# Attention and two gated MLPs on one core: odd query tiles transposed from key 0, groups of seven, and a planner given new priorities and buffer counts

## The chip, the cores and the metric

The kernel runs on one core of a Trainium2 chip. The metric is the device time of one execution in microseconds; the median of several executions is compared. All inputs and outputs are float32.

## What is computed

The first part is attention with a top-32 mask: 4 batches, 8 heads, 576 positions, head size 64. The result, 2304 tokens of 512 features, goes through two gated MLPs (512 to 1536 and back), one after the other.

```python
scores = scale * np.matmul(q, k.transpose(0, 1, 3, 2))
kth = np.partition(scores, -top_k, axis=-1)[..., -top_k:-top_k + 1]
attn = exp(where(scores >= kth, scores, -1e9) - max); attn /= sum + 1e-9
x = matmul(attn, v)                       # (B, H, S, D) -> (B*S, H*D)
x = (silu(x @ w_gate) * (x @ w_val)) @ w_out          # MLP 1
x = (sigmoid(x @ w_gate2) * (x @ w_val2)) @ w_out2    # MLP 2
```

## The kernel before

The 36 tiles of 64 queries (nine for each batch) are dealt to six chunks of 4, 5, 6, 7, 7 and 7 tiles. For each chunk comes `attention(c)` and then `moe(c)`, which runs both MLPs on the chunk's tokens, transposed (features on partitions, 256 to 448 tokens as columns). A chunk that crosses a batch boundary has two segments: chunk 3 has 3 + 4 tiles, chunk 4 has 5 + 2, chunk 5 has 7 of one batch.

**Attention.** Heads are taken in pairs. A unit of work is one pair of query tiles (m = 2, 128 queries, head 0 and head 1 beside each other in the row of `p`) or, where a group has an odd number, one single tile (m = 1), whose 128 partitions are 64 queries of head 0 and below them 64 queries of head 1. For each unit TensorE makes scores (`ps_s`), ScalarE copies them to `s`, VectorE finds the 32nd largest value of each row by four `max` and three `match_replace` steps (`top_full`), exponentials and mask follow (`row_tile`), and the rows are divided by their sum (`norm`, ScalarE or GpSimd). Then `turned` transposes the probabilities `p` in blocks of 128 keys on TensorE into `ps_t` (two buffers), and ScalarE copies them into `pt`, of which there is one buffer, nine blocks of 128 keys by up to 64 x `GMAX` queries. `pv` then multiplies `pt` with the values, ten matmuls for one group of up to `GMAX` tiles, and ScalarE copies the result to `x32`.

For a single tile, `turned` is called three times. The first two calls transpose four blocks each, head 0's from key 0 and head 1's from key 64, and each is copied out by one instruction that takes only that head's 64 columns of the block. The third call turns the last 64 keys of head 0 and the first 64 of head 1, 64 columns wide, with two small copies; one of these already reads partitions 0 to 63 and writes 64 to 127. There are 16 single tiles (chunks 1, 3, 4 and 5, four head pairs each) and 64 double ones. `groups` cuts a segment of seven tiles into 2 + 5, since `GMAX` is 6.

**MLPs.** Chunk 0 uses float32 weights (mode N), which `decode` rebuilds from packed 64-bit input (`wr` buffers, result `wf`, also stored to DRAM as `sw`). The other chunks (mode P) load `sw` into `raw` and split it into a high and a low part, `w` (ScalarE or GpSimd for the high one, GpSimd or VectorE for the low one); each product is then three matmuls (both parts of `w` with `xh`, and the high part of `w` with `xl`).

**Order of the work.** Nothing is scheduled by hand. Each operation is handed to `Plan` with its engine (or a choice of engines), an estimated duration, its inputs, the buffers that it needs, and a priority (smaller goes first, then program order). `Plan.run` simulates the engines with these numbers, and the order in which it starts the operations is the order in which they are issued, on every engine and on SP's DMA queue. Buffers of a ring are handed out in program order. The scores of chunk 5 are made early, in the time of chunks 0 and 1 (`early`, `E_IN`), stored to DRAM and loaded later. The constants ahead of the program are priorities (`P_...`, `NA`, `NP`, `HP`, `E_DMA`) and buffer counts (`WR`, `RAW`, `SIL`, `H32`, `WK`, `KR_RING`).

Of the kernel before, what the change touches and what calls it, by code (L numbers as in the profile page):

```python
# [18 lines left out]
P = 128  # L19
B, H, S, D = 4, 8, 576, 64  # L20
# [19 lines left out]
E_STEP = 0  # L40
E_SKIP = 2
E_LAST = 1
E_IN = [2, 1, 0, 0, 0, 0]
BEFORE = [1, 0, 0, 0, 0, 0]
WR = 4
P_CUT = 0
E_PRIO = 2
E_DMA = 5
SP = 4
WU = 3  # L50
KE = 2
HP = 2
DL = 6
NA = 0
NP = 1
P_ROUND = 5
P_MASK = 1
P_DEC = 2
P_MM = 3
P_QK = 2  # L60
P_K = 1
P_PT = 2
P_PV = 1
P_EX = 2
P_S = 1
P_X = 1
P_HH = 2
P_HL = 0
PT = 1
RAW = 3  # L70
WF = 16
W = 4
SIL = 3
H32 = 2
WK = 2
E_RING = 2
P_RING = 2
Q_RING = 2
K_RING = 2
KS_RING = 1  # L80
QS_RING = 1
KR_RING = 2
V_RING = 2
GMAX = 6
S_RING = 4
DMA_LAT = 2010.0
DEBUG = False
# [199 lines left out]
def act(n):  # L287
    return 5 + 1.18 * n
# [27 lines left out]
def attn_moe_kernel(ctx: ExitStack, tc, qT, kT, qD, kD, vL, wall, outT):  # L316
# [25 lines left out]
    def phase_pool(n, name, bufs):  # L342
# [16 lines left out]
        "x32": ring("x32", [P, NPAIR, S], F32, 1),  # L359
        "sil": ring("sil", [P, HW], F32, SIL),  # L360
        "h32": ring("h32", [P, HW], F32, H32),
        "s": ring("s", [P, 2, 2, 288], F32, S_RING),
        "st": ring("st", [P, 36], F32, 2 * S_RING + 2),
        "wk": ring("wk", [P, 2, 288], F32, WK),
        "e": ring("e", [P, S], F32, E_RING),
        "p": ring("p", [P, 2 * S], F32, P_RING),
        "pt": ring("pt", [P, 9, 64 * GMAX], F32, PT),
        "v": ring("v", [P, 10, D], F32, V_RING),
# [6 lines left out]
    for n in SIZES:  # L375
        g = sum(SIZES[:len(chunks)])
        segs = []
        for b in range(g // QT, (g + n - 1) // QT + 1):
            lo, hi = max(g, b * QT), min(g + n, (b + 1) * QT)
# [5 lines left out]
    for n in sorted(set(PHASE)):  # L385
# [3 lines left out]
        if "N" in kinds:  # L389
            T = max(SIZES[c] for c in mine if MODES[c] == "N") * 64  # L390
            specs.update(xn=([P, ND, T], F32, 2), hn=([P, NF, T], F32, 1), wr=([P, 512, 2], I32, WR),
                         wf=([P, 512], F32, WF), wu=([P, 512], I32, WU), wg=([P, 128], I32, 2))
# [5 lines left out]
        if kinds - {"N"}:  # L398
            specs["raw"] = ([P, 512], F32, RAW)
            specs["w"] = ([P, 2, 8, P], F32R, W)  # L400
        if n == 0:
            specs.update(q=([P, S], F32, Q_RING), k=([P, S], F32, K_RING))
        if n == PHASE[-1]:
            Q = 128 * max(x for y in chunks[NAT:] for _, _, x in y[2])
            specs.update(qr=([P, Q], F32, 1), qs=([P, Q], F32R, QS_RING), kr=([P, S], F32, KR_RING),
                         kh=([P, S], F32R, 2 * KS_RING), kl=([P, S], F32R, 2 * KS_RING))
# [21 lines left out]
    def f32(ap):  # L428
        return ap.bitcast(F32)

    def new(name, label=""):
        r = R[name]
        return Gen(r, f"{name if isinstance(name, str) else name[0]}_{len(r.gens)}{label}")
# [12 lines left out]
    def split_ops(hi, lo, raw, n, uses, deps, pa, pp, allocs=(), lo_raw=None, lo_hi=None):  # L446
# [7 lines left out]
        def f_lo(eng):  # L454
            (nc.gpsimd if eng == "pool" else nc.vector).tensor_sub(lo(), (lo_raw or raw)(), lo_hi() if lo_hi else f32(hi()))  # L455
        a = op({"act": (act(n), pa), "pool": (76 + n, pa + HP)}, 0, f_hi, deps=deps, uses=uses, allocs=allocs)
        b = op({"pool": (pool_tt(n), pp), "dve": (dve(n), DL)}, 0, f_lo, deps=[a], uses=list(uses) + list(allocs),
# [102 lines left out]
    def early():  # L560
        for c, on in enumerate(EARLY):
            for p in range(int(on)):
                for b, q0, n_s in chunks[c][2]:
                    kg, qg = new(("ke", 0)), new(("qe", 0))
                    lds = [load(kg, kT[b * NPAIR + p], n_bytes=P * S * 4, prio=E_DMA),
                           load(qg, qT[b * NPAIR + p, :, q0 * 64:(q0 + n_s) * 64], dst=lambda g, n=n_s: g[:, :n * 64],
                                n_bytes=P * n_s * 256, prio=E_DMA)]
                    for _, jp, m in pairs(q0, n_s):
# [3 lines left out]
    def early_pair(c, p, b, j, kg, qg, lds, o, m):  # L572
# [4 lines left out]
        def st():  # L577
            nc.sync.dma_start(scr, sg[:, :m])
        scr_s[p, b, j] = scr, op("dma", dma(P * S * 4 * m), st, deps=done, uses=[sg], prio=E_DMA, lat=DMA_LAT)

# [30 lines left out]
    def stacked_scores(sg, kq, o, m):  # L611
        keys, qs, deps, n = kq
        done = []
        for x in range(2):
            psg = new("ps_s")

            def qk(x=x, psg=psg):
                take(psg)
                for h in range(2):
                    at = o * 64 + (h * n * 64 + h * 64 * (n % 2) if m == 2 else 0)  # L620
                    for i in range(2):
                        nc.tensor.matmul(psg[:, h, :288], qs[:, at:at + P], keys[h][i][:, x * 288:x * 288 + 288],  # L622
                                         start=(i == 0), stop=(i == 1))
            a = op("pe", pe(4, 288), qk, deps=deps, uses=[qs] + [g for y in keys for g in y], allocs=[psg], prio=P_QK)
            done += to_sbuf(sg, [sg], psg, a, x, m, P_S)
        return done
# [78 lines left out]
    def segment(c, p, b, q0, n_s, x32g, col):  # L705
        bp = b * NPAIR + p
        kg = kq = None
        if p >= int(EARLY[c]) and (c > NAT or c == NAT and p >= NATP):
            kq = stacked(bp, q0, n_s)
        elif p >= int(EARLY[c]):  # L710
            kg, qg = new(("k", 0)), new(("q", 0))
            lds = [load(kg, kT[bp], n_bytes=P * S * 4, prio=1),
                   load(qg, qT[bp, :, q0 * 64:(q0 + n_s) * 64], dst=lambda g: g[:, :n_s * 64],
                        n_bytes=P * n_s * 256, prio=1)]
        vg = new("v")
        v_ld = load(vg, vL[bp], n_bytes=P * 2560, prio=3)
        adds = []
        off = 0
        for n in groups(n_s):
            ptg = new("pt")  # L720
            pt_ops = []
            for jp in range((n + 1) // 2):
                m = min(2, n - 2 * jp)
                pg, sg = new("p"), new("s")
                o = off + 2 * jp
                if kq is not None:
                    done = stacked_scores(sg, kq, o, m)
                elif kg is None:
                    done = [score_load(sg, m, *scr_s[p, b, q0 + o])]
                else:  # L730
                    done = score_ops(sg, [sg], kg, qg, lds, o, m, P_QK, P_S)
                norms = [row_tile(sg, new("st"), done, e, pg, BEFORE[c]) for e in range(m)]
                tiles[0] += 1
                if tiles[0] > E_SKIP:
                    step(E_IN[c])
                for k3 in range(3):
                    pt_ops += turned(pg, norms, ptg, 2 * jp * 64, k3, m)
            adds.append(pv(ptg, pt_ops, vg, v_ld, n, p, x32g, col))
            off += n
            col += n * 64  # L740
        return adds
# [7 lines left out]
    def row_tile(sg, stg, a, e, pg, before):  # L749
# [58 lines left out]
        y = op("dve", 75, inv, deps=[y], uses=[stg], prio=P_MASK)  # L808
        return op({"act": (act(S), NA), "pool": (700, NP)}, 0, norm, deps=[y], uses=[pg, stg])

# [24 lines left out]
    def turned(pg, norms, ptg, c0, k3, m):  # L835


        tg = new("ps_t")
        h = 64 * (m - 1) + 64
        if k3 < 2:  # L840
            o = [64 * k3 + (S * k3 if m == 2 else 0) + i * P for i in range(4)]
            deps = [norms[k3 if m == 2 else 0]]
            parts = [(lambda: ptg[:, 4 * k3:4 * k3 + 4, c0:c0 + h],
                      lambda: tg[:, :, 64 * k3:64 * k3 + 64] if m == 1 else tg[:], 4 * h)]
            width = P
        elif m == 2:
            o, deps, width = [512], norms, P
            parts = [(lambda: ptg[:, 8, c0:c0 + h], lambda: tg[:, 0], h)]
        else:
            o, deps, width = [512, 0], norms, 64  # L850
            parts = [(lambda e=e: ptg[64 * e:64 * e + 64, 8, c0:c0 + h],
                      lambda e=e: tg[:64, e, 64 * e:64 * e + 64], h) for e in range(2)]

        def tr():
            take(tg)
            for i, a in enumerate(o):
                nc.tensor.transpose(tg[:width, i], pg[:, a:a + width], ident)  # L857
        t = op("pe", 5 + pe(len(o), 128), tr, deps=deps, uses=[pg], allocs=[tg], prio=P_PT)
        out = []
        for dst, src, n in parts:  # L860
            def cp(dst=dst, src=src):
                take(ptg)
                nc.scalar.activation(out=dst(), in_=src(), func=AF.Copy)  # L863
            out.append(op("act", act_ps(n), cp, deps=[t], uses=[tg], allocs=[ptg], prio=P_PT))
        return out

    def pv(ptg, pt_ops, vg, v_ld, n, p, x32g, col):
# [4 lines left out]
        def go():  # L872
            take(og)
            for i in range(5):
                for h in range(2):
                    nc.tensor.matmul(og[64 * h:64 * h + 64, :W], vg[:, 8 + h if i == 4 else 4 * h + i],  # L876
                                     ptg[:, 8 if i == 4 else 4 * h + i, :W], start=(i == 0), stop=(i == 4))
        a = op("pe", 200 + 10 * max(W / 1.2 + 3, 110), go, deps=pt_ops + [v_ld], uses=[ptg, vg], allocs=[og], prio=P_PV)

# [16 lines left out]
    def moe(c):  # L896
# [20 lines left out]
        for moe_i in range(2):  # L917
            hs_g = [new(("hn", ph))] if nat else [new(("hh", ph)), new(("hl", ph))]
            h_ops = {}
            for f in range(NF):  # L920
# [4 lines left out]
                for gv in range(2):  # L925
                    blk, wg, w_ready = w[gv]
                    for o, n in halves:
# [5 lines left out]
                        deps = w_ready + ([y for x in x_ready for y in x] if f == 0 else [])  # L933
                        m = op("pe", pe_t(n), mm, deps=deps, uses=[wg] + xs, allocs=[pg], prio=P_MM)
                        if gv == 0:
# [22 lines left out]
                        def mul(pg=pg, sg=sg, h32=h32, n=n, moe_i=moe_i):  # L958
# [6 lines left out]
                                                lambda h32=h32, n=n: h32[:, :n], n,  # L965
                                                [h32], [v], P_HH, P_HL, allocs=[hh, hl])
            if moe_i == 0:
# [3 lines left out]
            for hs in range(12):  # L971
# [4 lines left out]
                for o, n in halves:  # L976
# [7 lines left out]
                    deps = w_ready + [prev] + [y for d in range(4) for y in h_ops[4 * s3 + d, o]]  # L984
                    m = op("pe", pe_t(n), mm, deps=deps, uses=[wg] + hs_g, allocs=[pg], prio=P_MM)
                    accs[o] = pg, m
# [96 lines left out]
```

## Time and profile before

| | |
|---|---|
| median of 3 executions | 1300.52 us (1300.29 to 1302.53) |
| the profiled execution | 1302.69 us |
| its span, first to last instruction | 1300.9 us |
| mean granted TensorE clock | 0.978 |
| busy: TensorE (PE) / its weight loads (PEld) | 1241.8 us / 1062.6 us |
| busy: VectorE (DVE) / GpSimd (POOL) / ScalarE (ACT) | 1110.6 us / 862.7 us / 837.5 us |

PE, PEld, DVE, ACT and POOL are the names in the profile; SP is the engine that issues all DMAs. L857 is line 857 of the kernel. TensorE's busy time is modelled, since matmuls overlap; its weight loads run beside them.

### The profile page before, as it was taken

What the parts mean: (1) busy time and instruction counts of PE and PEld (TensorE: products, weight loads), DVE (VectorE), ACT (ScalarE), POOL (GpSimd) and SP (SyncE); (2) the same over time, 40 slices, a digit from 0 to 9 for tenths busy, and PEclk for the clock granted to TensorE, in tenths of its full rate; (3) what the DMA queues carried; (4) which work ended last, traced back from release to release, by engine and by line L of the source; (5) the groups of instructions that cost most, each with busy time, mean ns of one, the idle gap of its engine ahead of it and who ended that gap; (6) DMA issues with size and microseconds to landing.
All of it is one profiled execution on the core that took longest, in us unless ns stands there. A gap on an engine that the chain in (4) does not pass through costs nothing.

```text
span 1300.9 us, 21941 instructions
## 1 busy us (share of the span) xinstructions
PE 1241.8 (95%) x7240; PEld 1062.6 (82%) x7240; DVE 1110.6 (85%) x2345; ACT 837.5 (64%) x1662; POOL 862.7 (66%) x853
## 2 busy tenths in 40 slices
PE   4677999998999999999999999999999999999998
PEld 1233677877899999999998988989889889999998
DVE  7899999899999989999999999999999965364441
ACT  6876889777877878767778676656555543332331
POOL 5633465646999999978898886777677654333341
PEclk9867999999999999999999999999999999999999
DMA  8772788885444454453444343445444223333332
GB/s 283 264 263 97 227 277 284 268 297 191 160 133 152 147 162 142 142 165 122 133 136 158 123 150 101 132 144 163 136 145 139 86 90 120 119 106 105 113 98 69
DMA packets 101202, 206.34 MB, mean 159 GB/s; under 512 B 12256, under 2 KB 21856, under 8 KB 101088
## 3 DMA queue, kind: packets, MB, share of 16 engines
q1 hardware_dynamic: 101088, 204.94, 48.7%
q8 instruction: 57, 0.93, 0.3%
q14 instruction: 57, 0.47, 0.1%
HBM read 173.05 MB, written 31.85 MB: 158 GB/s over the span
## 4 chain that ended last, share of the span: by engine, by line
PE 73%; DVE 9%; ACT 7%; DMA 4%; POOL 4%; issue 2%; SPq 0%; ACTq 0%; POOLq 0%; DVEq 0%
PE ps_m L911 58%; PE ps_t L857 5%; PE ps_v L876 5%; DVE st L824 3%; DMA wr<-in_wall_dram 3%; DVE wk L826 3%; PE ps_s L639 3%; PE ps_s L622 2%; DVE p L789 2%; DMA raw<-sw 1%; ACT wf L469 1%; ACT wg L484 1%; ACT s L649 1%; POOL w L455 1%; POOL wu L488 1%
## 5 line engine op out<-in xcount | busy, mean ns | idle before, releaser
L455 POOL TENSOR_TENSOR w<-raw,w 128x512 fp32r<-128x512 f32 x309 | 419.5, 1368 | 41.2 <-ACT w L450 31.9
L911 PE MATMUL ps_m<-xh,w 128*128 128x448 f32 (+2 forms) x1920 | 405.2, 353 | 0.4 <-POOL w L455 0.4
L911 PEld LDWEIGHTS ps_m<-xh,w 128*128 128x128 f32 x1920 | 337.5, 189 | 20.5 <-issue 1.5
L824 DVE MAX8 st<-wk 128x8 f32<-128x576 f32 x432 | 313.3, 745 | 0.0
L450 ACT ACTIVATE w<-raw 128x512 fp32r<-128x512 f32 x263 | 163.6, 628 | 172.4 <-PE ps_m L911 122.1
L911 PE MATMUL ps_m<-xl,w 128*128 128x448 f32 (+2 forms) x960 | 218.5, 349 | 0.0
L826 DVE MATCH_REPLACE8 wk<-st,wk 128x576 f32<-128x576 f32 x288 | 212.8, 739 | 0.0
L911 PE MATMUL ps_m<-hh,w 128*128 128x448 f32 (+2 forms) x960 | 201.7, 352 | 0.0
L452 POOL TENSOR_SCALAR w<-raw 128x512 fp32r<-128x512 f32 x97 | 64.1, 661 | 176.4 <-DMA raw<-sw 87.2
L911 PEld LDWEIGHTS ps_m<-xl,w 128*128 128x128 f32 x960 | 172.6, 188 | 9.7
L911 PEld LDWEIGHTS ps_m<-hh,w 128*128 128x128 f32 x960 | 168.6, 188 | 10.1 <-issue 0.9
L789 DVE SCALAR_TENSOR_TENSOR p<-s,st,e 128x576 f32<-128x576 f32 x128 | 145.3, 1135 | 0.0
L857 PE MATMUL ps_t<-ident,p 128*128 128x128 f32 (+1 forms) x736 | 116.2, 288 | 12.0 <-ACT p L802 9.0
L857 PEld LDWEIGHTS ps_t<-ident,p 128*128 128x128 f32 (+1 forms) x736 | 89.7, 145 | 42.5 <-ACT p L802 19.1
L863 ACT ACTIVATE pt<-ps_t 128x512 f32<-128x512 f32 (+3 forms) x256 | 106.6, 438 | 21.6 <-PE ps_t L857 20.0
L940 ACT ACTIVATE sil<-ps_m 128x448 f32<-128x448 f32 (+3 forms) x144 | 70.1, 487 | 70.5 <-PE ps_m L911 69.5
L824 DVE MAX8 st<-s 128x8 f32<-128x576 f32 x144 | 106.8, 743 | 8.0 <-ACT s L649 8.0
L455 DVE TENSOR_TENSOR w<-raw,w 128x512 fp32r<-128x512 f32 x51 | 53.9, 1058 | 65.5 <-POOL w L452 45.6
L911 PE MATMUL ps_m<-hl,w 128*128 128x448 f32 (+2 forms) x480 | 109.3, 349 | 0.0
L826 DVE MATCH_REPLACE8 wk<-st,s 128x576 f32<-128x576 f32 x144 | 106.5, 739 | 0.0
L802 ACT ACTIVATE p<-p,st 128x576 f32<-128x576 f32 x116 | 89.4, 771 | 22.2 <-DVE st L797 21.5
L777 ACT ACTIVATE e<-s,st 128x576 f32<-128x576 f32 x128 | 99.1, 774 | 3.1 <-POOL st L760 1.3
(70 smaller groups left out, 1804.5 us busy)
## 6 DMA issues: line engine op xcount, KB each, us to landing
raw<-sw SPq DMA_DIRECT2D x360, 256.0 KB, 2.8
wr<-in_wall_dram SPq DMA_DIRECT2D x72, 512.0 KB, 4.8
sw<-wf SPq DMA_DIRECT2D x72, 256.0 KB, 4.6
kr<-in_kD_dram SPq DMA_DIRECT2D x38, 288.0 KB, 2.9
v<-in_vL_dram SPq DMA_DIRECT2D x32, 320.0 KB, 3.3
ss<-se SPq DMA_DIRECT2D x12, 576.0 KB, 3.8
s<-ss SPq DMA_DIRECT2D x12, 576.0 KB, 4.2
out_dram<-h SPq DMA_DIRECT2D x12, 224.0 KB, 2.5
```

The source lines that it names most:

```text
L450: nc.scalar.activation(out=hi(), in_=raw(), func=AF.Copy)
L455: (nc.gpsimd if eng == "pool" else nc.vector).tensor_sub(lo(), (lo_raw or raw)(), lo_hi() if lo_hi else f32(hi()))
L777: nc.scalar.activation(out=eg[:], in_=src(), func=AF.Exp, bias=stg[:, 32:33], scale=SCALE)
L789: nc.vector.scalar_tensor_tensor(out=o, in0=src(), scalar=stg[:, 31:32], in1=eg[:], op0=ALU.is_ge, op1=ALU.mult, accum_out=stg[:, 33:34])
L802: nc.scalar.activation(out=o, in_=o, func=AF.Copy, scale=stg[:, 35:36])
L824: nc.vector.max(out=stg[:, 4 * k:4 * k + 8], in_=src() if k == 0 else wk())
L826: nc.vector.match_replace(out=wk(), in_to_replace=stg[:, 4 * k - 4:4 * k + 4], in_values=src() if k == 1 else wk(), imm_value=NEG)
L857: nc.tensor.transpose(tg[:width, i], pg[:, a:a + width], ident)
L863: nc.scalar.activation(out=dst(), in_=src(), func=AF.Copy)
L876: nc.tensor.matmul(og[64 * h:64 * h + 64, :W], vg[:, 8 + h if i == 4 else 4 * h + i], ptg[:, 8 if i == 4 else 4 * h + i, :W], start=(i == ...
L911: nc.tensor.matmul(pg[:, :n], blk(a, d), src(x, d), start=first and i == 0, stop=last and i == 4 * len(terms) - 1)
L940: nc.scalar.activation(out=sg[:, :n], in_=pg[:, :n], func=AF.Tanh, scale=0.5)
```

## The change

1. A single tile is turned in two calls instead of three. The first transposes four blocks of 128 keys, from key 0, for both heads at once; the second the last 64 keys. Head 1's blocks now begin 64 keys earlier than its places in `pt`, so its halves go out by copies that move 64 partitions up or down: four copies after the first call, two after the second.
2. `GMAX` is 7, so chunk 5's seven tiles are one group.
3. Priorities and buffer counts of the planner are other ones.

```diff
-E_IN = [2, 1, 0, 0, 0, 0]
+E_IN = [2, 2, 0, 0, 0, 0]
-WR = 4
+WR = 3
-E_DMA = 5
+E_DMA = 4
-HP = 2
+HP = 3
-NA = 0
-NP = 1
+NA = 1
+NP = 2
-P_MM = 3
-P_QK = 2
+P_MM = 4
+P_QK = 3
-P_PV = 1
+P_PV = 0
-P_S = 1
+P_S = 0
-P_HH = 2
-P_HL = 0
+P_HH = 0
+P_HL = 2
-RAW = 3
+RAW = 5
-SIL = 3
-H32 = 2
-WK = 2
+SIL = 4
+H32 = 3
+WK = 3
-KR_RING = 2
+KR_RING = 1
-GMAX = 6
+GMAX = 7
...
-                for k3 in range(3):
+                for k3 in range(m + 1):
                     pt_ops += turned(pg, norms, ptg, 2 * jp * 64, k3, m)
...
         tg = new("ps_t")
...
+        if m == 2:
...
         else:
-            o, deps, width = [512, 0], norms, 64
-            parts = [(lambda e=e: ptg[64 * e:64 * e + 64, 8, c0:c0 + h],
-                      lambda e=e: tg[:64, e, 64 * e:64 * e + 64], h) for e in range(2)]
+            h, deps = 64, norms
+            lo, up = slice(0, 64), slice(64, P)
+            if k3 == 0:
+                o, width = [i * P for i in range(4)], P
+                parts = [(lambda: ptg[:, 0:4, c0:c0 + h], lambda: tg[:, :, :64], 4 * h),
+                         (lambda: ptg[lo, 4:8, c0:c0 + h], lambda: tg[up, :, 64:], 4 * h),
+                         (lambda: ptg[up, 4:7, c0:c0 + h], lambda: tg[lo, 1:4, 64:], 3 * h),
+                         (lambda: ptg[up, 8, c0:c0 + h], lambda: tg[lo, 0, 64:], h)]
+            else:
+                o, width = [512], 64
+                parts = [(lambda: ptg[up, 7, c0:c0 + h], lambda: tg[lo, 0, 64:], h),
+                         (lambda: ptg[lo, 8, c0:c0 + h], lambda: tg[lo, 0, :64], h)]
```

## Rows read from the trace of the kernel before

**Rows 1.** Windows, five stretches: length, busy PE PEld DVE ACT POOL (instructions), clock, DMA share, GB/s.
```profile
8.00:131.00 123.00, 84.14 (x532) 33.09 (x532) 113.55 (x242) 93.08 (x187) 59.73 (x75) 0.78 0.65 226
131.00:300.00 169.00, 165.67 (x903) 126.53 (x900) 159.57 (x339) 140.32 (x271) 88.29 (x120) 1.00 0.81 269
300.00:600.00 300.00, 292.47 (x1952) 273.84 (x1952) 291.29 (x661) 231.44 (x476) 269.49 (x234) 0.99 0.48 151
600.00:1065.00 465.00, 464.71 (x2714) 416.70 (x2714) 442.98 (x982) 299.55 (x606) 361.49 (x338) 1.00 0.42 133
1065.00:1297.00 232.00, 231.99 (x1132) 211.80 (x1128) 103.18 (x125) 70.03 (x121) 82.57 (x81) 1.00 0.32 104
```

**Rows 2.** The page: the chain that ended last, shares of the span by engine.
```profile
PE 73%; DVE 9%; ACT 7%; DMA 4%; POOL 4%; issue 2%; SPq 0%; ACTq 0%; POOLq 0%; DVEq 0%
```

**Rows 3.** Timeline of PE, chunk 5's last single tile: start, duration, engine, line, what.
```profile
1044.91 0.98 PE L911 MATMUL ps_m<-xl,w 128*128 128x448 f32 x4
1045.73 0.60 PE L857 MATMUL ps_t<-ident,p 128*128 128x128 f32 x4
1046.09 1.87 PE L911 MATMUL ps_m<-xh,w 128*128 128x448 f32 x8
1047.79 0.98 PE L911 MATMUL ps_m<-xl,w 128*128 128x448 f32 x4
1048.61 1.78 PE L911 MATMUL ps_m<-xh,w 128*128 128x448 f32 x8
...
1055.63 0.97 PE L911 MATMUL ps_m<-xl,w 128*128 128x448 f32 x4
1056.43 1.03 PE L857 MATMUL ps_t<-ident,p 128*128 128x128 f32 x8
1057.22 1.90 PE L911 MATMUL ps_m<-xh,w 128*128 128x448 f32 x8
1058.96 0.99 PE L911 MATMUL ps_m<-xl,w 128*128 128x448 f32 x4
1059.78 0.38 PE L857 MATMUL ps_t<-ident,p 128*64 128x128 f32 x2
1059.92 1.89 PE L911 MATMUL ps_m<-xh,w 128*128 128x448 f32 x8
```

**Rows 4.** Timeline of PE, two groups of p v in chunk 5's attention.
```profile
854.79 2.91 PE L876 MATMUL ps_v<-pt,v 128*64 128x320 f32 x20
857.64 0.66 PE L857 MATMUL ps_t<-ident,p 128*128 128x128 f32 x4
...
866.05 1.31 PE L876 MATMUL ps_v<-pt,v 128*64 128x128 f32 x20
867.30 1.88 PE L911 MATMUL ps_m<-xh,w 128*128 128x448 f32 x8
```

**Rows 5.** Groups by shape, whole span: count, busy, mean ns of one, idle before.
```profile
L857 PE MATMUL ps_t<-ident,p 128*128 128x128 f32 x704 | 110.4, 289 | 11.8 <-ACT p L802 9.0 <-POOL p L804 2.0 <-ACT pt L863 0.2
L863 ACT ACTIVATE pt<-ps_t 128x256 f32<-128x256 f32 x32 | 11.1, 379 | 2.7 <-PE ps_t L857 2.5
L863 ACT ACTIVATE pt<-ps_t 64x64 f32<-64x64 f32 x32 | 6.7, 211 | 1.9 <-PE ps_t L857 1.7
```

**Rows 6.** Groups by shape, 600 to 1065 us.
```profile
L857 PE MATMUL ps_t<-ident,p 128*64 128x128 f32 x18 | 3.4, 272 | 0.0
```

**Rows 7.** Tile `wr`, 131 to 310 us: readers, min/median/max ns, first and last start.
```profile
L469 ACT ACTIVATE wf<-wr x56: 649/678/717, 135.1 to 283.9; 128x512 f32<-128x512 f32 x56
L484 ACT ACTIVATE wg<-wr x52: 644/672/702, 140.4 to 280.2; 128x512 int8<-128x512 int16 x52
L496 POOL TENSOR_SCALAR wu<-wr x31: 762/778/1189, 142.0 to 282.0; 128x512 uint8<-128x512 uint8 x31
...
DMA to landing us min/median/max: 3.3/4.6/6.9
```

**Rows 8.** Waits of SP's DMA queue: us in total, times, longest us.
```profile
SPq L443 <- POOL w L455: 538.4, 281, 7.1
```

More of the change, by code (lines that the diff above doesn't have):

```diff
@@ L838, in turned @@
         tg = new("ps_t")
[L839 to L844, printed above, removed]
+        if m == 2:
+            h, deps = P, norms if k3 == 2 else [norms[k3]]
+            if k3 < 2:
+                o = [64 * k3 + S * k3 + i * P for i in range(4)]
+                parts = [(lambda: ptg[:, 4 * k3:4 * k3 + 4, c0:c0 + h], lambda: tg[:], 4 * h)]
+            else:
+                o = [512]
+                parts = [(lambda: ptg[:, 8, c0:c0 + h], lambda: tg[:, 0], h)]
             width = P
-        elif m == 2:
-            o, deps, width = [512], norms, P
-            parts = [(lambda: ptg[:, 8, c0:c0 + h], lambda: tg[:, 0], h)]
-        else:
-            o, deps, width = [512, 0], norms, 64
-            parts = [(lambda e=e: ptg[64 * e:64 * e + 64, 8, c0:c0 + h],
-                      lambda e=e: tg[:64, e, 64 * e:64 * e + 64], h) for e in range(2)]
+        else:
+            h, deps = 64, norms
[6 more added lines that the diff above has]
+                         (lambda: ptg[up, 8, c0:c0 + h], lambda: tg[lo, 0, 64:], h)]
+            else:
+                o, width = [512], 64
+                parts = [(lambda: ptg[up, 7, c0:c0 + h], lambda: tg[lo, 0, 64:], h),
+                         (lambda: ptg[lo, 8, c0:c0 + h], lambda: tg[lo, 0, :64], h)]
         def tr():
```

## The prediction

> **What bounds the kernel now.** I read the chain that ended last, then the busy time by stretch, then single places of TensorE's timeline. The chain is TensorE for 73% of the span [rows 2], so what matters is where TensorE is truly full, and where it waits. The windows tell that [rows 1]. From 1065 us on there is only MLP work: TensorE is busy 231.99 of 232 us and loads weights in 211.80 of them, 91%. From 600 to 1065 us, with attention and MLP mixed, it is busy 464.71 of 465 us and loads weights in 90%: it is as full there as where nothing else is asked of it. From 300 to 600 us it idles 7.5 us, from 131 to 300 us 3.3 us, and from 8 to 131 us 38.9 us; in that stretch chunk 0's attention hangs on VectorE (113.55 of 123 us) and TensorE's mean granted clock is 0.78, so some of its work there ran at 1.2 GHz instead of 2.4. VectorE is busy 97% of the time from 300 to 600 us and 95% from 600 to 1065, then 44%. When its attention work ends at 1065 us, TensorE still has 232 us of MLP matmuls ahead, of which chunk 5's are only a part. VectorE is thus early in the end, TensorE is not: a microsecond of TensorE's work removed after 131 us should shorten the run by nearly a microsecond.
>
> **Transposes of single tiles.** The timeline shows what a transpose takes from the matmuls around it [rows 3]. Undisturbed, a group's last four matmuls (xl) are followed by the next group 0.82 us later (1047.79 to 1048.61). With four transposes between, the next group comes at 1046.09 instead of 1044.91 + 0.82 = 1045.73: 0.36 us, 0.09 each. The single tile's eight cost 1057.22 - (1055.63 + 0.82) = 0.77 us, its two narrow ones 1059.92 - (1058.96 + 0.82) = 0.14 us. Before: 0.91 us for a single tile. After: four (0.36) and one narrow (0.07), 0.43 us. Saved 0.48 us, for 16 single tiles 7.7 us. Bounds: the mean of all transposes, 110.4 us / 704 = 0.157 us, waits and the slow clock included [rows 5], gives 80 x 0.157 = 12.6 us above. Below, only the tiles that stand where TensorE is full count: there are 18 narrow transposes after 600 us [rows 6], two for each tile, so nine tiles: 4.3 us. I take 7.7, since the idle left in the two earlier stretches is 2 to 3% of them.
>
> **Copies out of ps_t.** A single tile had two copies of 128x256 (0.379 us each) and two of 64x64 (0.211 us) [rows 5], 1.18 us. It gets one of 128x256, one of 64x256, one of 64x192 and three of 64x64. The two new shapes lie between 0.211 and 0.379 us, since the rows hold a smaller copy and one with as many columns; I take 0.38 and 0.33, being nearer to the longer in columns. That is 0.38 + 0.38 + 0.33 + 0.63 = 1.72 us, 0.54 more, 8.6 us for 16 tiles (bounds 0.25 to 0.59 each, 4 to 9.4 us in all). That a copy moves partitions costs nothing that the rows could show: half of the 64x64 copies already do so, in a group with one mean. ScalarE is busy 140 of 169 us from 131 to 300 us and 64% from 600 to 1065 us [rows 1], so its own idle time takes this up. `pv` waits for the copies, and the next unit needs their `ps_t` buffers; the planner puts groups of MLP matmuls of about 2.5 us between the pieces (1057.22 to 1059.78), which hide 0.54 us more. Were that cover gone, TensorE would stand 16 x 0.54 = 8.6 us, and the gain of the transposes were spent. I take 0.
>
> **Groups of seven.** Chunk 5 has 2 + 5 tiles in two groups for each head pair: 1.25 us (866.05 to 867.30) for 128 columns and 2.85 us (854.79 to 857.64) for 320 [rows 4]. The difference is 0.00833 us for a column, so 448 columns take 3.92 us: 0.18 us saved, four times, 0.7 us. Bounds: 0, and 4 x 1.25 = 5 us if the short group's columns rode along free; the slope from the rows speaks for the lower end. `pt` is handed over once instead of twice for a pair, the first half of it is held longer; that costs only where TensorE has nothing else to do, which does not happen after 600 us.
>
> **Priorities and buffers.** No instruction is added or removed by them. Rings are handed out in program order, so the order of scores, transposes and MLP groups among themselves stays, and only their interleaving moves. `E_IN` makes the last four early score units come two to a tile in chunk 1. On TensorE transposes now precede scores; on ScalarE `hh` and the score copies come sooner, the norms later; GpSimd gets the low parts of `h` later and fewer high parts of `w`. What hides all this is that TensorE has MLP groups ready. With `RAW` 5, two more weight loads may be under way: SP's queue waited 538 us for GpSimd to give back a buffer of `raw` [rows 8], and what stands behind a waiting load in that queue waits too (keys, values, stored scores). That can only relieve. `KR_RING` 1 goes against it: the second head's keys load only once the first head's are split. The cover is the ring of four score tiles that VectorE still has to search; without it, each of the 19 segments that use `kr` would lose at most about one landing, 4.6 us taken from the larger load of rows 7, 87 us of VectorE's time in all, of which TensorE's stock of MLP work absorbs a part. I cost both at 0. `SIL`, `H32` and `WK` with one buffer more relieve waits; at best the order gains back the idle of 38.9 + 3.3 + 7.5 = 50 us in rows 1, at worst it adds waits of its own. With no row for either I take 0 for the order as a whole, and keep both ends for the range.
>
> **Sum.** 7.7 + 0.7 = 8.4 us. The profiled execution took 1302.7 us (span 1300.9); less 8.4 that is 1294.3. It lies 2.2 us above the median of the runs shown, 1300.5, so the median should come to 1292.
>
> **Rival 1, the weights of chunk 0 run dry (slower).** Place: 131 to 300 us, mode N, where DMA is busy 81% and TensorE hardly idles [rows 1]. `WR` falls from 4 to 3. A buffer is held from the issue of its load to its last reader: 4.6 us to land, then 0.68, 0.67 and 0.78 us for the three readers, and the step between them, which I take as long as the last: at least 7.5 us [rows 7]. With three buffers that is one half slab every 2.5 us. Needed are 52 between 140.4 and 280.2 us [rows 7], one every 2.7 us. It just fits; it decides from a hold of 8.1 us on. With 9 us it is 3.0 us each, 52 x 0.3 = 16 us longer, and 1300.5 - 8.4 + 16 = 1308. For it: landings of up to 6.9 us. Against it: 16 decoded half slabs wait in `wf` when the stage begins, and fewer loads under way may land sooner.
>
> **Rival 2, VectorE is the bound (no change).** Its 97% from 300 to 600 us, in places of which the MLP's own VectorE steps queue behind the search, would turn TensorE's saving into idle time; the result is 1300.5. Against it speaks the full TensorE after 600 us. The Trainium skill (Perfetto Trace Analysis, Identifying the Most-Contended Engine) says that matmul busy time misleads, that TensorE is to be judged by its weight loads and the other engines by occupancy, the highest being the one to optimize. By that rule VectorE's 95% stands above TensorE's 90% from 600 to 1065 us, and this change would touch the wrong engine: 1300.5 instead of 1292. The trace does not bear that out, since 91% is all that weight loads reach where TensorE alone works.
>
> **Rival 3, the new order pays too (faster).** If a quarter of the 50 us of idle comes back, most of it ahead of 131 us, the result is 1292 - 12 = 1280.
>
> **How the numbers follow.** Forecast 0.50, within 1286 to 1297 by the bounds above (12.6 us saved; or 4.3). Rival 1, with the other ways in which the order may lose, 0.19; rival 2, or an order that gives back just what is saved, 0.13; rival 3, 0.18. A difference of 0.2%, 2.6 us, is about what a measurement of this kernel can tell from none. Faster: 0.50 + 0.18 = 0.68; same 0.13; slower 0.19. The range takes in most of rivals 1 and 3: 1277 to 1309, with about 1 in 10 left out on either side.
>
> **What would show it.** Right: 656 transposes instead of 736, 288 copies of 0.2 to 0.6 us out of `ps_t`, four p v groups of 448 columns at 3.9 us, TensorE's busy time down by some 8 us, idle unchanged ahead of 600 us and none after, and the last attention piece still some 230 us ahead of the end. Rival 1: waits of ScalarE for `wr` landings, and the mode N stage longer than 169 us. Rival 2: TensorE idle between 300 and 1065 us. Rival 3: the first MLP matmul earlier than 131 us. The forecast is wrong above all if the order changes more than the counted work does, in either direction.

## The result and the profile after

The changed kernel takes 1290.1 us (median of 4 executions, 1289.3 to 1294.4) where the kernel before, in the same comparison, takes 1301.5: ratio 0.9906, 95% interval 0.9886 to 0.9925, that is 12 us (10 to 15) less. Measured once more beside other kernels it gave 0.9886 (0.9868 to 0.9904). The forecast was 8.4 us less, 1292, in 1277 to 1309.

The profiled execution took 1294.35 us, the slowest of the four, with a span of 1292.5 us: 8.4 us less than the span of before. That this equals the sum is luck, as the stages show below.

First the page's chain of the changed kernel, and its windows over the stretches of [rows 1] (length, busy PE, PEld, DVE, ACT, POOL, clock, DMA share, GB/s).

```profile
PE 79%; DMA 7%; ACT 6%; DVE 3%; POOL 3%; issue 2%; SPq 0%; POOLq 0%; ACTq 0%; DVEq 0%
```

```profile
8.00:131.00 123.00, 82.88 (x533) 34.12 (x534) 112.06 (x241) 90.24 (x186) 61.91 (x78) 0.83 0.65 220
131.00:300.00 169.00, 162.18 (x873) 122.84 (x873) 152.94 (x323) 135.48 (x265) 93.17 (x126) 0.99 0.85 264
300.00:600.00 300.00, 294.01 (x1952) 274.55 (x1952) 291.85 (x669) 238.41 (x501) 268.59 (x235) 0.99 0.52 157
600.00:1065.00 465.00, 465.00 (x2621) 414.16 (x2620) 439.44 (x983) 297.54 (x612) 375.94 (x353) 1.00 0.44 135
```

Against [rows 2] the chain has more of TensorE (79% for 73) and less of VectorE (3% for 9), but also more of DMA (7% for 4). From 600 to 1065 us TensorE has no idle left; from 131 to 300 us it idles 6.8 us, twice as much as in [rows 1].

The groups by shape answer to [rows 5] (count, busy, mean ns of one, idle before).

```profile
L866 PE MATMUL ps_t<-ident,p 128*128 128x128 f32 x640 | 101.6, 288 | 9.0 <-ACT p L802 6.8 <-POOL p L804 2.1
L885 PE MATMUL ps_v<-pt,v 128*64 128x448 f32 x80 | 15.9, 544 | 0.0
L872 ACT ACTIVATE pt<-ps_t 64x64 f32<-64x64 f32 x48 | 8.5, 211 | 0.5
L872 ACT ACTIVATE pt<-ps_t 64x256 f32<-64x256 f32 x16 | 6.1, 381 | 0.4
L872 ACT ACTIVATE pt<-ps_t 128x256 f32<-128x256 f32 x16 | 6.0, 375 | 0.3 <-PE ps_t L866 0.2
L872 ACT ACTIVATE pt<-ps_t 64x192 f32<-64x192 f32 x16 | 5.2, 323 | 0.2
```

TensorE's timeline at chunk 5's last single tile and its group of seven answers to [rows 3, 4].

```profile
1054.21 0.98 PE L920 MATMUL ps_m<-xl,w 128*128 128x448 f32 x4
1055.03 1.78 PE L920 MATMUL ps_m<-xh,w 128*128 128x448 f32 x8
1056.65 0.97 PE L920 MATMUL ps_m<-xl,w 128*128 128x448 f32 x4
1057.46 0.71 PE L866 MATMUL ps_t<-ident,p 128*128 128x128 f32 x5
1057.92 1.85 PE L920 MATMUL ps_m<-xh,w 128*128 128x448 f32 x8
1059.62 0.98 PE L920 MATMUL ps_m<-xl,w 128*128 128x448 f32 x4
1060.52 3.98 PE L885 MATMUL ps_v<-pt,v 128*64 128x448 f32 x20
1064.43 1.91 PE L920 MATMUL ps_m<-xh,w 128*128 128x448 f32 x8
1066.18 0.99 PE L920 MATMUL ps_m<-xl,w 128*128 128x448 f32 x4
```

Read as in the prediction, a single tile now takes 1057.92 - (1056.65 + 0.82) = 0.45 us of TensorE (forecast 0.43, before 0.91), the group of seven 3.91 us (forecast 3.92). The new copies take 0.381 and 0.323 us (forecast 0.38 and 0.33), and moving 64 partitions costs nothing that shows: each 64x64 copy takes 0.20 to 0.23 us, whether it moves or not.

That reading of TensorE stops too early, where the next MLP group starts. The group behind the transposes is itself longer: in [rows 3] its xl matmuls come 1.70 us after its start (1046.09 to 1047.79), undisturbed 1.62 (1048.61 to 1050.23). The whole price shows from one group's xl matmuls to the next group's. Two lines of the kernel before that [rows 3] does not have:

```profile
1050.23 0.97 PE L911 MATMUL ps_m<-xl,w 128*128 128x448 f32 x4
...
1061.65 0.99 PE L911 MATMUL ps_m<-xl,w 128*128 128x448 f32 x4
```

Undisturbed that is 2.44 us (1047.79 to 1050.23). With the eight wide transposes it was 3.33 (1055.63 to 1058.96) and with the two narrow ones 2.69 (1058.96 to 1061.65), 1.14 us more together; now it is 2.97 (1056.65 to 1059.62), 0.53 more. The medians of such places, 3.31, 2.66 and 2.98 us against about 2.45 undisturbed, make the saving 0.55 us a tile, not 0.46. Read the same way, the p v groups of 128 and 320 columns took 3.88 - 2.45 = 1.43 and 5.51 - 2.45 = 3.06 us, and the group of 448 takes 6.56 - 2.45 = 4.11 (1059.62 to 1066.18): 0.4 us saved for each of the four head pairs, 1.5 in all.

The tile `wr`, 131 to 310 us, answers to [rows 7] (reader, min/median/max ns, first and last start; then what its readers waited for, in us and times).

```profile
L469 ACT ACTIVATE wf<-wr x56: 655/678/703, 130.9 to 292.2; 128x512 f32<-128x512 f32 x56
L443 SPq DMA_DIRECT2D wr<-in_wall_dram x53: 327/332/377, 131.6 to 285.7; - x53
...
  DMA wr<-in_wall_dram: 25.5, 20
...
DMA to landing us min/median/max: 3.6/5.2/7.4
```

Its readers wait 25.5 us for landings (7.6 us in 11 places in the kernel before), and the last `wf` copy starts at 292.2 us instead of 283.9.

**Two halves of the run.** TensorE's timeline gives the moment of the first MLP matmul, that of the first one of 320 columns (the first of chunk 1, when the packed weights are through), and the time from there to the last matmul. The last 1056 of the 4896 MLP matmuls, which come after all attention work in every kernel, have a column of their own. All kernels of this study stand here:

| kernel | first MLP matmul | first of 320 columns | from there to the end | of that, the last 1056 MLP matmuls | ratio to before (95%) |
|---|---|---|---|---|---|
| before | 131.2 | 309.9 | 987.5 | 217.0 | 1 |
| changed | 128.6 | 312.1 | 976.8 | 217.0 | 0.9906 (0.9886 to 0.9925) |
| changed, again | 127.7 | 307.5 | 977.2 | 217.0 | 0.9886 (0.9868 to 0.9904) |
| turning alone | 130.0 | 303.5 | 982.7 | 214.5 | 0.9927 (0.9911 to 0.9944) |
| sevens alone | 130.7 | 308.9 | 984.2 | 217.0 | 0.9988 (0.9976 to 0.9999) |
| both, old constants | 132.3 | 306.9 | 980.3 | 217.1 | 0.9918 (0.9902 to 0.9934) |
| constants alone | 125.0 | 306.4 | 982.5 | 214.5 | 0.9946 (0.9934 to 0.9958) |
| buffer counts alone | 127.2 | 318.3 | 980.3 | 217.0 | 1.0016 (1.0005 to 1.0028) |
| priorities alone | 129.1 | 314.5 | 982.3 | 216.2 | 1.0021 (1.0009 to 1.0033) |
| changed, transposes twice | 125.8 | 303.0 | 983.9 | 217.0 | 0.9933 (0.9918 to 0.9948) |
| changed, transposes four times | 126.7 | 308.3 | 995.3 | 216.2 | 1.0051 (1.0038 to 1.0064) |
| changed, copies twice | 125.1 | 308.4 | 982.7 | 216.2 | 0.9955 (0.9940 to 0.9971) |
| changed, WR 4 laid out anew | 129.7 | 304.7 | 980.5 | 217.0 | 0.9926 (0.9910 to 0.9941) |
| changed, WR 4 in the same order | 126.9 | 299.7 | 976.5 | 217.0 | 0.9840 (0.9819 to 0.9860) |

The part behind the first matmul of 320 columns repeats to 0.7 us in the changed order (976.8, 977.2; 976.5 with a fourth buffer). The part ahead of it does not: the five traces with the changed order and three buffers reach that point between 303.0 and 312.1 us, and the executions of one kernel spread too (1284.0 to 1290.6 us for the changed kernel measured again). So the later part is compared by traces, the earlier by the ratios and by several traces.

The last 1056 matmuls are the same work in every kernel, yet take 217, 216.2 or 214.5 us, at a granted clock of 1.00. The timeline shows two paces: from one group's hl matmuls (those with the low part of `h`) to the next group's it is 2.47 us in the kernel before and 2.43 with the constants alone (first two lines: before).

```profile
1106.85 0.99 PE L911 MATMUL ps_m<-hl,w 128*128 128x448 f32 x4
1109.32 0.99 PE L911 MATMUL ps_m<-hl,w 128*128 128x448 f32 x4
```

```profile
1107.65 0.97 PE L911 MATMUL ps_m<-hl,w 128*128 128x448 f32 x4
1110.08 0.97 PE L911 MATMUL ps_m<-hl,w 128*128 128x448 f32 x4
```

What sets the pace stays open; it is not the order, since kernels with the changed order have 217.0 and 216.2. So the gains behind the 320-column point are compared below without these matmuls, in what is called the shared stretch: 987.5 - 217.0 = 770.5 us before, 760.0 us in the changed kernel.

### The profile page after: what moved, and what is told of

Same layout as the page of the kernel before. It is cut to its first block, busy times and chain, and to the rows that moved or that the text cites. A ratio compares the mean times of both kernels' runs of the same rounds, so it can differ in the third digit from the quotient of the medians.

```text
span 1292.5 us, 21608 instructions
## 1 busy us (share of the span) xinstructions
PE 1230.5 (95%) x7080; PEld 1050.6 (81%) x7080; DVE 1105.2 (86%) x2330; ACT 829.4 (64%) x1675; POOL 898.6 (70%) x883
## 4 chain that ended last, share of the span: by engine, by line
PE 79%; DMA 7%; ACT 6%; DVE 3%; POOL 3%; issue 2%; SPq 0%; POOLq 0%; ACTq 0%; DVEq 0%
PE ps_m L920 63%; DMA wr<-in_wall_dram 6%; PE ps_v L885 6%; PE ps_t L866 5%; PE ps_s L622 3%; PE ps_s L639 2%; DVE st L824 1%; ACT wf L469 1%; DVE wk L826 1%; ACT wg L484 1%; POOL wu L488 1%; POOL wu L496 1%; ACT s L649 1%; ACT wu L494 1%; POOL e L768 0%
## 5 line engine op out<-in xcount | busy, mean ns | idle before, releaser
L455 POOL TENSOR_TENSOR w<-raw,w 128x512 fp32r<-128x512 f32 x314 | 436.5, 1403 | 12.3 <-ACT w L450 6.2
L450 ACT ACTIVATE w<-raw 128x512 fp32r<-128x512 f32 x242 | 148.5, 629 | 175.4 <-PE ps_m L920 129.4
L452 POOL TENSOR_SCALAR w<-raw 128x512 fp32r<-128x512 f32 x118 | 76.1, 646 | 174.0 <-PE ps_m L920 160.3
L920 PEld LDWEIGHTS ps_m<-hh,w 128*128 128x128 f32 x960 | 168.7, 188 | 10.3 <-issue 1.2
L789 DVE SCALAR_TENSOR_TENSOR p<-s,st,e 128x576 f32<-128x576 f32 x128 | 137.2, 1072 | 0.0
L872 ACT ACTIVATE pt<-ps_t 128x512 f32<-128x512 f32 (+4 forms) x288 | 112.1, 418 | 14.9 <-PE ps_t L866 12.9
L866 PE MATMUL ps_t<-ident,p 128*128 128x128 f32 x656 | 103.4, 288 | 9.0 <-ACT p L802 6.8
L866 PEld LDWEIGHTS ps_t<-ident,p 128*128 128x128 f32 x656 | 80.7, 146 | 37.2 <-ACT p L802 13.2
L488 POOL TENSOR_SCALAR wu<-wg 128x512 int8<-128x512 int8 x72 | 62.2, 865 | 68.6 <-ACT wg L484 64.9
L455 POOL TENSOR_TENSOR hl<-h,hh 128x448 fp32r<-128x448 f32 (+2 forms) x92 | 102.7, 1117 | 2.0 <-ACT hh L450 1.4
```

Of the source, the lines that this page charges most:

```text
L450: nc.scalar.activation(out=hi(), in_=raw(), func=AF.Copy)
L452: nc.gpsimd.tensor_scalar(hi(), raw(), 1.0, 1.0, op0=ALU.mult, op1=ALU.mult)
L488: nc.gpsimd.tensor_scalar(parts(u, I8, 4)[:, :, 3], g[:].bitcast(I8), 64.0, -64.0, op0=ALU.mult, op1=ALU.add)
L789: nc.vector.scalar_tensor_tensor(out=o, in0=src(), scalar=stg[:, 31:32], in1=eg[:], op0=ALU.is_ge, op1=ALU.mult, accum_out=stg[:, 33:34])
L920: nc.tensor.matmul(pg[:, :n], blk(a, d), src(x, d), start=first and i == 0, stop=last and i == 4 * len(terms) - 1)
```

## The experiments

**The parts one by one.** The theory was that TensorE's counted work makes the gain and the order is neutral; the rivals, that the order makes it, or that VectorE is the bound and nothing comes of it.

Turning alone, on the kernel before: the three calls and the copies of the diff, no constant.

> The kernel before with the new way of turning single tiles alone (old priorities and buffer counts, groups of at most six). Theory (TensorE's work counts): 80 transposes fewer at 0.09 us, 7.7 us less, ratio 0.994 against the kernel before, within 0.002 since the planner lays the work out anew. Rival (the new priorities and buffers made the gain): 1.000. Rival (VectorE is the bound): 1.000.

Groups of seven alone:

```diff
-GMAX = 6
+GMAX = 7
```

> The kernel before with groups of seven alone. Theory: 0.7 us less, ratio 0.999 to 1.000, not to be told from no change. Rival (handing over the single buffer pt less often pays): 3 us or more, ratio 0.998 or below.

Both, with the old constants:

> The kernel before with the new turning and groups of seven, old priorities and buffer counts. Theory: the whole counted work, 8.4 us less, ratio 0.9935. What the changed kernel gained beyond that (it measured 0.9906, 12 us) would be the order's. Rival (the order made the gain): 1.000.

All new constants but `GMAX`, with the old turning:

> The kernel before with all the new priorities and buffer counts, but the old turning and groups of at most six. Theory (the order is neutral, what moved is TensorE's work): ratio 1.000, within 0.003. Rival (the order made the gain): 0.991 to 0.994. Rival (three buffers for the packed weights make the stage of float32 weights longer): 1.003 or more, with the stage from the first MLP matmul to the first matmul of 320 columns longer than the 178.7 us of before.

Measured: 0.9927, 0.9988, 0.9918 and 0.9946. The first three come out a little above the theory, with 9.5, 1.6 and 10.7 us for 7.7, 0.7 and 8.4; by the whole price of the section above the work is 16 x 0.55 = 8.8, 1.5 and 10.3. The fourth does not fit: 7.0 us from an order that I had put at nothing.

By stage the totals are less tidy. In the shared stretch both changes with the old constants save 770.5 - 763.2 = 7.3 us, and the new constants on top of them 763.2 - 760.0 = 3.2 more; the constants alone save 2.5 there. The rest of their 7.0 lies in the pace of the last 1056 matmuls (2.5) and ahead of the 320-column point, where one trace says little. Turning alone saves only 2.3 us in the shared stretch, where twelve of its sixteen tiles (12 x 0.55 = 6.6) stand: its new layout lost some of that, and its total agrees with the theory partly by luck. The parts don't add either, 10.7 and 7.0 against 12 to 15 together, but each has an interval of some 2 us either way.

One place where the order costs TensorE time is in the windows from 545 to 600 us, in the kernel before and, below, with the constants alone.

```profile
545.00:600.00 55.00, 53.09 (x349) 48.81 (x348) 55.00 (x123) 39.85 (x87) 44.30 (x42) 1.00 0.44 135
```

```profile
545.00:600.00 55.00, 54.84 (x362) 51.76 (x361) 52.92 (x122) 37.86 (x78) 47.50 (x47) 1.00 0.47 145
```

At the change from one MLP to the next in chunk 2, TensorE of the kernel before loads weights in 48.8 of 55 us, with VectorE busy all the time; with the constants alone it is 51.8, with turning alone 52.0, in the changed kernel 52.3. The same 240 MLP matmuls there (the 1681st to the 1920th) take 62.3 us before and 58.3 with the constants alone, with 51 transposes between them in both. Of the 3.0 us that the two windows differ by in weight loads, matmul busy time shows only 1.8 (53.09 to 54.84), so [rows 1], where I counted idle by busy time, understated the loss. The Trainium skill (Perfetto Trace Analysis, Identifying the Most-Contended Engine) says that matmul busy time is a bad measure for TensorE, and that its weight loads, beside the share of peak arithmetic, are the better one. In this stretch the trace agrees.

**Is it any new layout, or these constants?** Buffer counts alone and priorities alone, on the kernel before:

```diff
# buffer counts alone
-WR = 4
+WR = 3
-RAW = 3
+RAW = 5
-SIL, H32, WK = 3, 2, 2
+SIL, H32, WK = 4, 3, 3
-KR_RING = 2
+KR_RING = 1
```

> The kernel before with the new buffer counts alone (WR, RAW, SIL, H32, WK, KR_RING). All new constants together gave 0.9946. Theory (the gain is TensorE's lost time from 545 to 600 us, which any other layout of the work avoids): about 0.995 to 0.997, as with the priorities. Rival (the deeper rings for weights make the gain): 0.9946 here and 1.000 with the priorities.

The other constants (E_IN, E_DMA, HP, NA, NP, P_...), with the old buffer counts:

> The kernel before with the new priorities alone (P_..., NA, NP, HP, E_DMA and E_IN). Theory (any other layout avoids the loss from 545 to 600 us): 0.995 to 0.997. Rival (the rings make the gain): 1.000. Rival (the priorities make it): 0.9946 here and 1.000 with the rings.

Measured 1.0016 and 1.0021: neither theory, and neither rival as put. The table parts it. In the shared stretch both save, 770.5 - 763.3 = 7.2 and 4.4 us, more than the constants together (2.5); the sevens alone save 3.3, of which 1.5 is work, and turning alone less than its work. So a new layout mostly avoids the loss there, but by how much differs by several us from one layout to the next. Both kernels reach the 320-column point late, at 318.3 and 314.5 us in one trace each, and give it all back. Why the two sets do not add up, ahead of that point or behind it, was not taken apart further.

**What a transpose costs.** In the changed kernel each transpose of a single tile is issued two or four times into the same place; the planner is told nothing, so the order stays.

```diff
-            for i, a in enumerate(o):
+            for i, a in list(enumerate(o)) * (3 - m):      # four times: (7 - 3 * m)
```

> The changed kernel with each transpose of a single tile issued twice into the same place; the planner is told nothing of it, so the order and the choice of engines stay. 80 transposes more, 64 wide and 16 narrow ones. Theory (TensorE is full): 64 x 0.09 + 16 x 0.07 = 6.9 us more than the changed kernel, ratio 0.996 against the kernel before instead of 0.9906. Rival (VectorE is the bound, TensorE has room): as the changed kernel, 0.9906.

> The changed kernel with each transpose of a single tile issued four times into the same place, the planner told nothing: 240 transposes more. Theory (TensorE is full, 0.09 us for a wide one and 0.07 for a narrow one): 20.7 us more than the changed kernel, ratio about 1.0065, and 13/16 of it, 17 us, after the first matmul of 320 columns. Rival (half of them fall into waits of TensorE): 10 us, 0.998. Rival (VectorE is the bound): 0.9906.

Four times: 1.0051, and 0.9886 for the changed kernel measured beside it, 0.0165 x 1302.5 = 21.5 us for 240 transposes (some 3 us either way), 0.090 us each. Twice: 0.9933, 4 to 6 us more for 6.9 expected. Twelve of the sixteen single tiles, not thirteen as the expectation has it, come after the first matmul of 320 columns in every trace. In the shared stretch four times costs 779.1 - 760.0 = 19.1 us for 12/16 x 20.7 = 15.5 expected, and twice 6.9 us for 5.2: 0.106 to 0.115 us each. The period from xl to xl agrees with that. With the transposes of a single tile between, it is 2.98 us in the changed kernel, 3.56 with them twice and 4.62 with them four times, and 12 x 0.58 = 7.0 us, 12 x 1.64 = 19.7. So what is added to TensorE in the shared stretch counts in full, and VectorE, busy for 95% of the time from 600 to 1065 us against TensorE's 90% of weight loads, is not the bound there. The four tiles ahead of the 320-column point add little that could be told from the spread of that part. By the rule of the Trainium skill (Perfetto Trace Analysis, Identifying the Most-Contended Engine), to optimize the engine with the highest occupancy first, VectorE would have been the one; here the measurement decides against that.

**Do the copies cost anything?**

```diff
-                nc.scalar.activation(out=dst(), in_=src(), func=AF.Copy)
+                for _ in range(3 - m):
+                    nc.scalar.activation(out=dst(), in_=src(), func=AF.Copy)
```

> The changed kernel with each copy of a single tile out of ps_t issued twice, the planner told nothing. ScalarE gets 96 copies, 16 x 1.72 = 27 us, more. Theory (the copies lie in ScalarE's idle time): as the changed kernel, 0.9906, within 0.002. Rival (p v and the next transposes wait for them): up to 27 us more, 1.011; at a third of it 0.997.

Measured 0.9955, some 6 to 9 us more than the changed kernel, and 766.5 - 760.0 = 6.5 us in the shared stretch, for 12 x 1.72 = 20.6 us of copies there: a quarter to a third of their time. The waits show where, first with copies twice from 306 us on, then in the changed kernel from 310 us on (us in total, times, longest):

```profile
PEld ps_v L886 <- ACT pt L873: 5.4, 14, 1.0
...
PEld ps_t L866 <- ACT p L802: 5.0, 8, 1.5
```

```profile
PEld ps_v L885 <- ACT pt L872: 1.7, 6, 0.3
...
PEld ps_t L866 <- ACT p L802: 1.2, 2, 0.9
```

p v waits for the last copies into `pt`, and transposes wait longer for the rows that ScalarE divides (L802). The theory that the copies lie in idle time falls. Of the 8.6 us that the change adds, a quarter to a third would be 2 to 3 us, an estimate from the doubled copies; what the changed kernel's trace shows is 1.7 us of p v waiting for `pt`, and the kernel before has no such wait behind the 320-column point.

**Three or four buffers for the packed weights.** First with the planner laying out the work anew, then with its order for three kept and only the buffers on the chip four:

```diff
-WR = 3
+WR = 4
...
+    R["wr", 0].bufs = 3      # second kernel only: the planner still counts three
```

> The changed kernel with four buffers for the packed weights instead of three. Theory (the forecast's count: three just suffice): as the changed kernel, 0.9906, within 0.002. Rival (three starve the stage of float32 weights): the stage, 183.5 us in the changed kernel's trace and 178.7 us before, falls back by 4 to 5 us, ratio 0.987, and ScalarE's 23.5 us of waiting for landings of these weights go back to about 3 us.

> The changed kernel, laid out by the planner for three buffers of packed weights as before, but given four of them on the chip, so that only the waits for a free one change and not the order. Theory (three buffers starve the stage of float32 weights, and the kernel with four that was laid out anew lost elsewhere): that stage, 177 to 184 us in the traces with this order, comes to 175 us, ScalarE's 23 to 25 us of waiting for landings fall below 10, and the rest stays at 977 us; ratio 0.985 where the changed kernel has 0.989 to 0.991. Rival (the loads share one rate, more of them under way land later): as the changed kernel.

The first is inconclusive: the stage is shorter (175.0 us from the first MLP matmul to the 320-column point), but the new layout loses 763.5 - 760.0 = 3.5 us behind it, and 0.9926 is not below the changed kernel. The second settles it, since all its instructions run in the changed kernel's order: 0.984, 1281.9 us, 6 to 9 us less than the changed kernel and the fastest of the study. In its trace the stage takes 172.8 us, against 177.2 to 183.5 in the five traces with three buffers; the rest stays at 976.5 us. The tile `wr` again, 131 to 310 us:

```profile
L470 ACT ACTIVATE wf<-wr x55: 650/675/741, 131.2 to 279.6; 128x512 f32<-128x512 f32 x55
...
L444 SPq DMA_DIRECT2D wr<-in_wall_dram x52: 327/333/803, 131.5 to 273.6; - x52
...
  DMA wr<-in_wall_dram: 1.2, 2
...
DMA to landing us min/median/max: 3.2/5.4/7.8
```

A load lands no sooner (5.4 us for 5.2), but it is asked for sooner (the last at 273.6 us for 285.7), and the readers wait 1.2 us instead of 25.5.

The changed kernel once more:

> The changed kernel once more, beside the three others of this job. It measured 0.9906 (0.9886 to 0.9925); from the same program the same is expected, 0.989 to 0.993. By stage: TensorE's work after the first matmul of 320 columns takes the same time to 1 us (976.8 us in the trace at hand), what comes ahead of it moves by several us from run to run (312.1, 303.0 and 308.4 us in three runs with this order).

0.9886, as expected, with 977.2 us in the later part.

## Why the prediction was right, and where it was not

**What bounds it: right.** In the shared stretch TensorE's work counts one for one: 240 transposes added 21.5 us, 19.1 of them there, where 12 of the 16 tiles stand. Ahead of the 320-column point the spread of the traces hides what work costs.

**Transposes: right in kind, priced too low.** By the prediction's own reading a tile takes 0.45 us for 0.43 forecast. But that reading leaves out that the next MLP group runs longer too: over the whole period a tile took about 1.1 us before and 0.53 after, so 0.55 us are saved instead of 0.48, 8.8 us for 16 tiles instead of 7.7.

**Copies: mis-sized.** Their durations came out to 0.01 us, but I put their cost at 0, hidden by the MLP groups between the pieces. About 2 us show, as an estimate: p v waits 1.7 us for them, and a quarter to a third of the time of doubled copies came on top of the run.

**Groups of seven: right in kind.** By the prediction's reading 1.25 + 2.85 - 3.91 = 0.19 us a pair, 0.8 in all; over the whole period 0.4 us a pair, 1.5 in all, of 1.6 us measured with an interval of 1.5 either way.

**Priorities and buffers at 0: two errors of opposite sign.** First, the new constants are worth some 3 us in the shared stretch: 3.2 on top of the other two changes, 2.5 alone. The whole 10.5 us saved there are 12 x 0.55 + 1.5 = 8.1 of work, less about 2 for copies, plus these 3.2; the 1 us left over is not explained. I had the idle of the stretch in [rows 1] and no way to say that it would come back, and by weight loads the loss was larger than busy time shows. That a deeper `raw` ring could only relieve SP's queue did not show either: its wait for GpSimd there is 572.3 us, for 538.4 in [rows 8]. Second, rival 1's mechanism was real. I had worked out that three buffers just fit, with a hold of at least 7.5 us against a limit of 8.1 [rows 7]. Landings became slower (5.2 us median for 4.6), which by the same sum makes 8.1 us, the readers waited 25.5 us instead of 7.6, and three buffers cost 6 to 9 us. I had tied that to a slower kernel; it was paid out of what the new order gains ahead of 310 us: with four buffers in that order the one trace comes to the 320-column point at 299.7 us, 10 us earlier than before, and three give back 3 to 12 of it.

**The sum.** 8.4 us forecast, 12 to 15 measured, inside the range. That it lies so near is in part luck, as the work was worth some 10 us, the constants 3 more behind the 320-column point, the copies cost about 2, and what the order gained ahead of that point went mostly into the three buffers. TensorE's full stretch from 600 us on is as forecast, and its busy time fell by 11.3 us (1241.8 to 1230.5) for some 8 forecast. Its idle ahead of 600 us was not unchanged: 40.1, 6.8 and 6.0 us in the three stretches, for 38.9, 3.3 and 7.5. Signs of rivals 1 and 3 came too, the waits for `wr` and a first MLP matmul at 128.6 us instead of 131.2.

## What to carry to other kernels

Where one engine is full, work on it can be priced from its timeline, but over a whole period, from a point in one group to the same point in the next: the gap alone gave 0.46 us here where the period gave 0.55. The busy share of another engine said little against it. A retuned order is not neutral in such a kernel: judge it stage by stage, since a gain in one and a loss in another can cancel in the total. When a planner chooses a buffer count, try that order with one buffer more on the chip: the order may be good and the count not.

## What had not been expected of the hardware

The same order of work reaches the first matmul of 320 columns at 303.0 to 312.1 us in five traces (two of them of the changed kernel itself, at 312.1 and 307.5, three with work added for single tiles), while the shared stretch of the changed kernel repeats to 0.4 us. The mean granted clock from 8 to 131 us differs with it (0.83 and 0.79 in the changed kernel's two traces), but the later start of the two is the one with the higher clock; what sets that spread was not tried.

The last 1056 MLP matmuls, with nothing else on TensorE and a granted clock of 1.00, run at one of two paces, 2.48 or 2.43 us on average for a group of twelve of 448 columns. Two traces out of fourteen keep the faster pace for both MLPs, the others for only one of them. That makes up to 2.5 us of 1290 between kernels, without any change in that work.
